# Convolution and expert layer on one core: a reordered fill, one fp16 comparison for each one-hot matrix, front work moved between half rounds, and picks spread over the last round

## The chip, the cores and the metric

One core of one Trainium2 chip. The metric is the device time of one execution in microseconds (us), shorter is better. The profile is one execution, and its span is about 1.7 us shorter than the time of that same execution.

## The reference, cut to what matters

A causal depthwise convolution of width 7 with softmaxed weights per head, then a mixture of 8 experts with top-1 routing. 28,672 tokens (8 batches of 3584) of width 192; hidden width 1024.

```python
x_pad = concat([zeros((B, 6, D)), x], axis=1)
out = einsum('hk,bskhg->bshg', softmax(weight), windows(x_pad))   # 8 heads of 24
x = out.reshape(N, D)
logits = x @ w_gate
e_idx = argmax(logits, axis=1)
gate_w = softmax(logits)[arange(N), e_idx]
eom = sigmoid(x @ w_output_gate)
for e in range(8):
    mask = e_idx == e
    h = maximum(x[mask] @ w1[e], 0.0)
    out[mask] = gate_w[mask, None] * eom[mask, e, None] * (h @ w2[e])
```

## The kernel before

The tokens are worked through in 16 units of 1792. For each unit the *front* does, on TensorE, the convolution (8 head matmuls with a band matrix), transposes and gate logits; then the routing, which counts tokens by expert and finds each token's place in its expert's stream. A unit's rows are reordered by matmuls with one-hot matrices, 8 groups of two blocks, and scattered by GpSimd (POOL in the profile) into sorted rows in device memory. The *slots* then load 512 sorted rows of one expert, transposed by the DMA, and run the two expert matmuls; results go to the output by a scatter on GpSimd. One round of the main loop is four slots of unit u interleaved with the front of later units. Units 0 to 2 go through the front before the first slot: the fill. Front convolutions and groups share two PSUM buffers (`pf`).

The front's one-hot matrices, two comparisons each with a per-row scalar:

```python
        pos = pr.tile([128, NB], FP32, tag="pos", name="pos")
        nc.vector.tensor_reduce(out=pos[P], in_=dm[P], axis=AX.X, op=ALU.add)
        # ... five small operations for dd, R, dst, du; then
        def prep(i):
            # ... (for even i: the scaled rows xr of two groups)
            pms[i] = pp16.tile([128, 2, 256], FP16, tag="pm", name="pm")
            for l in range(2):
                nc.vector.tensor_scalar(out=pms[i][P, l, :], in0=pos16[P],
                                        scalar1=pos[P, l * NG + i:l * NG + i + 1],
                                        scalar2=None, op0=ALU.is_equal)
        prep(0)
        prep(1)
```

The scatter of a group, ordered behind everything but other scatters and loads, so also behind the *guard*, eight zero writes, each over the 512 rows at the head of one expert's stream:

```python
    def scatter(u, du, xs, i):
        i = nc.gpsimd.indirect_dma_start(out=xcg2, out_offset=...(ap=du[:, i:i + 1], axis=0),
                                         in_=xs..., ...)
        nodep(i, f"sc{u}", [f"sc{v}" for v in range(NU)] + ["load"])
```

The fill and the main loop:

```python
    for u in range(U0 + 1):                       # U0 = 2
        fa, fb = front_a(u + 1, u < U0), front_b(u)
        drain(fa, 1)
        while drain(fb, 1):
            drain(fa, 2 if u < U0 else 1)
            emit_in(len(pend))                    # issue the ready row scatters
        if u == 0:
            # ... rest of fa, weights of two experts, then the guard's zero writes
    # ...
    for u in range(U0, NU):
        # ... fs: groups of unit u+1; fa, fbn: front and routing of unit u+2
        for k, (w, inv, xabi) in enumerate(todo):
            # ... weights of a later expert; s: the slot
            for q in range(4):
                pos = 4 * k + q
                if q % 2 == 0:
                    s.first(q // 2)               # half a hidden layer
                drain(fa, 1)
                if prev is not None:
                    prev.second(q)                # an output quarter of the previous slot
                    emit_out()                    # its output scatters
                if pos < 8:
                    drain(fs, 1)
                elif pos < 12:
                    drain(fa, 1)
                else:
                    drain(fbn, 1)
                emit_in(len(pend))
                # ... at pos 7 the loads of the next round
```

Within `first` the last relu of a slot's hidden layer goes to VectorE (DVE), the other three to ScalarE (ACT):

```python
                if q == 3:
                    nc.vector.tensor_relu(out=ht, in_=pps[r])
                else:
                    nc.scalar.activation(out=ht, in_=pps[r], func=AF.Relu)
```

In the last round three extra slots are *picked* on the chip (15 small VectorE operations each), all three before the round begins.

## Time and profile before

| | before |
|---|---|
| median of 4 runs, us | 647.11 (646.61 to 647.94) |
| profiled span, us | 645.5 |
| mean granted TensorE clock | 0.981 |
| VectorE, ScalarE, GpSimd busy, us | 406.3, 355.4, 401.5 |

The prediction below shows the page's first part, the stretches and the waits. Where it speaks of half clock, the granted clock of this trace is 0.50, from 65 to 68 and from 90 to 94. For the comparison afterwards four instants matter, because they cut the execution at the same points of the work in every kernel: three of TensorE and the end. This is TensorE's timeline of the kernel before (start, duration, operation; in brackets the idle time before it and what ended it): the first slot's second load being used, and the gate logits of the first and of the last of the 12 units whose logits come in a round.

```profile
90.51 0.59 PE L613 MATMUL pp<-xb,wres 128*128 128x512 f16 x1 [0.74 <-DMA xb<-xcg_sorted]
...
119.38 1.73 PE L313 MATMUL pf<-tt,wg 128*32 128x448 f32 x16
...
535.38 1.71 PE L313 MATMUL pf<-tt,wg 128*32 128x448 f32 x16 [0.42 <-DVE tt L280]
```

So the fill ends at 90.51, the first logits follow 28.87 later, the 11 rounds take 416.00 (37.82 each), and the end 645.5 - 535.38 = 110.1. These four stages are the bookkeeping of this study.

### The profile page before, as it was taken

Reading aid. Unit: us, or ns where it says so; the run is one execution under the profiler, and the core shown is the slowest. Engines: PE = TensorE matmul, PEld = TensorE weight load, DVE = VectorE, ACT = ScalarE, POOL = GpSimd, SP = SyncE. Lnnn points to the kernel's source line nnn. Section 1 sums busy time; section 2 is a strip of 40 time slices with the busy share of each in tenths; the row PEclk is TensorE's granted clock in tenths of the full one; section 3 lists DMA queues with packets and bytes.
Section 4 is the critical chain, followed back from the end, with each engine's and each line's share of the span. In section 5 each row is a group of like instructions: output and inputs, shape, how many; then the busy total and the mean of one; then the engine's idle time right before and its main releaser. Section 6 shows DMA issues by size and latency. Waiting matters only on the chain.

```text
span 645.5 us, 13578 instructions
## 1 busy us (share of the span) xinstructions
PE 586.5 (91%) x4544; PEld 360.3 (56%) x4544; DVE 406.3 (63%) x1362; ACT 355.4 (55%) x586; POOL 401.5 (62%) x419
## 2 busy tenths in 40 slices
PE   3998739999999999999999999999999999979993
PEld 1554415656665566656566566655566565546662
DVE  7567536584957658494775849577594956943332
ACT  1676525554665555556555555555555565656661
POOL 1362726876775756667476655756566674777773
PEclk9999859999999999999999999999999999999997
DMA  6979439994654647264553637355372525246631
GB/s 160 191 186 258 132 76 201 143 211 137 138 169 117 176 106 171 85 153 131 117 155 101 185 87 165 105 114 165 92 188 88 107 82 113 73 108 136 188 115 37
DMA packets 162569, 88.14 MB, mean 137 GB/s; under 512 B 116765, under 2 KB 153792, under 8 KB 162496
## 3 DMA queue, kind: packets, MB, share of 16 engines
q1 hardware_dynamic: 131872, 43.92, 30.3%
q0 software_dynamic: 29728, 43.30, 25.8%
q8 instruction: 36, 0.59, 0.4%
q14 instruction: 37, 0.30, 0.2%
q10 hardware_dynamic: 896, 0.03, 0.1%
HBM read 35.92 MB, written 43.06 MB: 122 GB/s over the span
## 4 chain that ended last, share of the span: by engine, by line
PE 66%; DVE 19%; ACT 6%; DMA 4%; issue 3%; SPq 0%; POOL 0%; DVEq 0%; ACTq 0%; POOLq 0%
PE pyt L655 18%; PE pp L613 13%; PE pf L290 11%; PE pp L620 8%; PE pf L444 5%; DVE ht L631 5%; PE pf L313 5%; PE pf L304 5%; ACT ht L633 4%; DVE xrow L423 2%; DVE pm L428 2%; DVE cv L280 2%; PE pf L322 2%; DMA out_dram<-y,oi 1%; DMA xt<-in_x_dram 1%
## 5 line engine op out<-in xcount | busy, mean ns | idle before, releaser
L482 POOL DMA_INDIRECT out_dram<-y,oi x246 | 245.6, 998 | 127.6 <-ACT y L661 63.4
L633 ACT ACTIVATE ht<-pp 128x1024 f16<-128x1024 f32 (+1 forms) x189 | 183.1, 1001 | 69.8 <-PE pp L620 67.0
L655 PEld LDWEIGHTS <-ht 128*128 128x128 f16 x1968 | 166.6, 98 | 58.2 <-issue 29.5
L655 PE MATMUL pyt<-wres,ht 128*128 128x192 f16 x1920 | 192.7, 246 | 1.5 <-DVE ht L631 1.5
L462 POOL DMA_INDIRECT xcg_sorted<-xs,du x128 | 131.5, 1027 | 92.2 <-DVE tk L502 22.1
L290 PE MATMUL pf<-xt,band 118*112 118x384 f32 x256 | 109.4, 523 | 19.1 <-DMA xt<-in_x_dram 10.8
L631 DVE TENSOR_SCALAR ht<-pp 128x1024 f16<-128x1024 f32 (+1 forms) x63 | 74.7, 1185 | 71.8 <-PE pp L613 71.8
L661 ACT COPY y<-pyt 128x384 f32<-128x384 f32 x123 | 59.0, 479 | 85.6 <-PE pyt L655 84.1
L613 PE MATMUL pp<-xa,wres 128*128 128x512 f16 x240 | 92.9, 387 | 9.1 <-DMA xa<-xcg_sorted 9.1
L613 PE MATMUL pp<-xb,wres 128*128 128x512 f16 x240 | 91.3, 380 | 1.2 <-DMA xb<-xcg_sorted 1.2
L620 PE MATMUL pp<-xb,wres 64*128 64x512 f16 x240 | 73.0, 383 | 1.6 <-ACT ht L633 1.2
L620 PE MATMUL pp<-xa,wres 64*128 64x512 f16 x240 | 73.0, 383 | 0.0
L444 PE MATMUL pf<-xrow,pm 112*128 112x194 f16 x512 | 65.1, 249 | 5.8 <-DVE pm L428 4.1
L613 PEld LDWEIGHTS <-wres 128*128 128x128 f16 x480 | 34.8, 97 | 60.7 <-issue 59.7
L290 PEld LDWEIGHTS pf<-xt,band 118*112 118x112 f32 x256 | 42.5, 185 | 41.6 <-DVE cv L280 11.5
L278 ACT COPY cv<-pf 112x384 f32<-112x384 f32 x80 | 38.1, 478 | 46.5 <-PE pf L290 38.6
L428 DVE TENSOR_SCALAR pm<-pos,pos 112x256 f16<-112x256 f16 x256 | 62.1, 307 | 0.0
L423 DVE TENSOR_TENSOR xrow<-cv,gs 112x384 f16<-112x384 f32 x121 | 61.9, 551 | 0.0
L444 PEld LDWEIGHTS <-pm 112*128 112x128 f16 x512 | 44.7, 98 | 15.3 <-DVE pm L428 7.7
L304 PE MATMUL pf<-identf,cv 112*128 112x112 f32 x384 | 50.7, 260 | 2.3 <-ACT tt L278 2.1
L278 ACT CAST xs<-pf 128x388 f16<-128x388 f32 x76 | 37.1, 492 | 27.5 <-PE pf L444 27.5
L304 PEld LDWEIGHTS pf<-identf,cv 112*128 112x128 f32 x384 | 40.9, 141 | 10.0 <-ACT tt L278 3.4
(139 smaller groups left out, 447.2 us busy)
## 6 DMA issues: line engine op xcount, KB each, us to landing
xt<-in_x_dram SPq DMA_DIRECT2D x8, 1344.0 KB
xt<-in_x_dram SPq DMA_DIRECT2D x8, 1260.0 KB
out_dram<-y,oi POOLq DMA_INDIRECT x246
wres<-in_moe_w_dram POOLq DMA_DIRECT2D x8, 384.0 KB
wd<-wres SPq DMA_DIRECT2D x3, 768.0 KB
wres<-in_moe_w_dram POOLq DMA_DIRECT2D x8, 256.0 KB
xcg_sorted<-xs,du POOLq DMA_INDIRECT x128
xcg_sorted<-zrow SPq DMA_DIRECT2D x8, 256.0 KB
```

What stands on the lines that cost most here:

```text
L278: nc.scalar.copy(out=o, in_=i)
L290: nc.tensor.matmul(pc[0:BT, 0:NB * GH], band[0:KI, h, :], xt[0:KI, :, h * GH:(h + 1) * GH], start=True, stop=True)
L304: nc.tensor.matmul(pt[:, j * BT:(j + 1) * BT], cvf[0:BT, m * 2 * D + i * 128:m * 2 * D + (i + 1) * 128], identf[0:BT, 0:BT], is_transpose= ...
L428: nc.vector.tensor_scalar(out=pms[i][P, l, :], in0=pos16[P], scalar1=pos[P, l * NG + i:l * NG + i + 1], scalar2=None, op0=ALU.is_equal)
L444: nc.tensor.matmul(ps[:, r * XW:(r + 1) * XW], pm[P, l, r * 128:(r + 1) * 128], xr[P, l * NG + i, :], start=(r == 0 and l == 0), stop=(r = ...
L462: i = nc.gpsimd.indirect_dma_start(out=xcg2, out_offset=bass.IndirectOffsetOnAxis(ap=du[:, i:i + 1], axis=0), in_=xs.rearrange("p r w -> p ...
L482: i = nc.gpsimd.indirect_dma_start(out=out, out_offset=bass.IndirectOffsetOnAxis(ap=oi[:, j:j + 1], axis=0), in_=y[:, j, :], in_offset=Non ...
L613: nc.tensor.matmul(pps[r][:, l, :], w[:, o2:o2 + 128], x, start=(r == 0), stop=(r == 1))
L620: nc.tensor.matmul(pps[r][:, l, :], w[p0:p0 + 64, c:c + 128], x[p0:p0 + 64], start=(r == 1), stop=(r == 0))
L631: nc.vector.tensor_relu(out=ht, in_=pps[r])
L633: nc.scalar.activation(out=ht, in_=pps[r], func=AF.Relu)
L655: nc.tensor.matmul(self.pp[:, o:o + D], self.ht[fc // 2][:, fc % 2, q * 128:(q + 1) * 128], self.w[:, w:w + D], start=(fc == 0 and q % 2 = ...
```

## The change

Its intent: (1) let the row scatters of unit 1 go out while the guard is still being written, and give the fill an order in which the routing of a unit starts earlier; (2) build each one-hot matrix with one instruction in place of two; (3) lay the front's pieces out over the half rounds so that logits and their transposes are separated by matmul work, and choose the copying engine by place; (4) issue weights in single pieces; (5) make one pick per slot of the last round. The core of the diff (cuts marked with ...):

```diff
-        pos = pr.tile([128, NB], FP32, tag="pos", name="pos")
-        nc.vector.tensor_reduce(out=pos[P], in_=dm[P], axis=AX.X, op=ALU.add)
+        pos = pr.tile([128, NB], FP16, tag="pos", name="pos")
+        nc.vector.tensor_reduce(out=pos[P], in_=dm[P], axis=AX.X, op=ALU.max)
 ...
-            for l in range(2):
-                nc.vector.tensor_scalar(out=pms[i][P, l, :], in0=pos16[P],
-                                        scalar1=pos[P, l * NG + i:l * NG + i + 1],
-                                        scalar2=None, op0=ALU.is_equal)
+            nc.vector.tensor_tensor(
+                out=pms[i][P], in0=bass.AP(tensor=pos16.tensor, offset=pos16.offset,
+                                           ap=[[pos16.ap[0][0], BT], [0, 2], [1, 256]]),
+                in1=pos.rearrange("p (l i) -> p i l", l=2)[P, i, :].unsqueeze(2)
+                .to_broadcast([BT, 2, 256]), op=ALU.is_equal)
 ...   (prep(0) now stands ahead of the dd, R, dst, du operations, prep(1) behind them)
-        nodep(i, f"sc{u}", [f"sc{v}" for v in range(NU)] + ["load"])
+        nodep(i, f"sc{u}", [f"sc{v}" for v in range(NU)] + ["load", "guard"])
 ...   (fill)
         while drain(fb, 1):
-            drain(fa, 2 if u < U0 else 1)
+            n += 1
+            drain(fa, 1 if u == U0 or n > 8 else 2 if n < 8 else 0)
             emit_in(len(pend))
+            if u < U0 and n > 4 and n % 2:
+                load_w(1)
 ...   (round)
-                drain(fa, 1)
+                if pos in (0, 2, 4, 6, 8, 10, 12):
+                    evac_on[0] = "act" if pos < 8 else None
+                    drain(fa, 1)
+                if pos == 14:
+                    drain(fbn, 1)
                 if prev is not None:
                     prev.second(q)
                     emit_out()
+                if pos in (1, 3, 5, 7, 8, 9, 10, 11):
+                    evac_on[0] = "dve" if pos < 8 else None
+                    drain(fa, 2 if pos == 9 else 1)
                 if pos < 8:
+                    evac_on[0] = "act"
                     drain(fs, 1)
 ...
+                if u == NU - 1 and q == 3 and k < ND:
+                    todo.append(load_pick())
```

More of the change, by code (lines that the diff above doesn't have):

```diff
@@ L202, with w_pieces, load_w @@
     wres = const.tile([128, E * WE], FP16)
-    def load_w(e):
+    def w_pieces(e):
         o = e * WE
         w = moe_w1[e]
-        nc.gpsimd.dma_start(
-            wres[:, o:o + F].rearrange("p (l c) -> p l c", l=2),
-            bass.AP(tensor=w.tensor, offset=w.offset,
-                    ap=[[F, 128], [64 * F + F // 2, 2], [1, F // 2]]))
-        nc.gpsimd.dma_start(wres[0:64, o + F:o + WA], w[0:64, F // 2:F])
-        nc.gpsimd.dma_start(wres[64:128, o + F:o + WA], w[128:D, 0:F // 2])
-        nc.gpsimd.dma_start(
-            wres[:, o + WA:o + WE].rearrange("p (c d) -> p c d", d=D),
-            moe_w2[e].rearrange("(c p) d -> p c d", p=128))
+        return [
+            (wres[:, o:o + F].rearrange("p (l c) -> p l c", l=2),
+             bass.AP(tensor=w.tensor, offset=w.offset,
+                     ap=[[F, 128], [64 * F + F // 2, 2], [1, F // 2]])),
+            (wres[0:64, o + F:o + WA], w[0:64, F // 2:F]),
+            (wres[64:128, o + F:o + WA], w[128:D, 0:F // 2]),
+            (wres[:, o + WA:o + WE].rearrange("p (c d) -> p c d", d=D),
+             moe_w2[e].rearrange("(c p) d -> p c d", p=128))]
+    wq = deque(p for e in range(E) for p in w_pieces(e))
+    def load_w(n):
+        while n and wq:
+            nc.gpsimd.dma_start(*wq.popleft())
+            n -= 1
     GE = NG * E
@@ L273, in pft @@
         return pool.tile([128, 512], FP32, tag=tag, name="pf")
+    evac_on = [None]
     def evac(o, i):
         sync_flip[0] ^= 1
-        if sync_flip[0] or fill[0] is not None:
+        if evac_on[0] is not None:
+            act = evac_on[0] == "act"
+        else:
+            act = sync_flip[0] or fill[0] is not None
+        if act:
             nc.scalar.copy(out=o, in_=i)
@@ L391, in front_b @@
                                 in1=msk[P], op=ALU.mult)
-        pos = pr.tile([128, NB], FP32, tag="pos", name="pos")
-        nc.vector.tensor_reduce(out=pos[P], in_=dm[P], axis=AX.X, op=ALU.add)
-        dd = pr.tile([128, NG, E + 1], FP32, tag="dd", name="dd")
-        nc.vector.tensor_tensor(
-            out=dd, in0=pk[:, c0 + NSEG:c0 + 2 * NSEG].rearrange("p (i e) -> p i e", e=E + 1),
-            in1=bass.AP(tensor=R9.tensor, offset=R9.offset,
-                        ap=[list(R9.ap[0]), [0, NG], [1, E + 1]]), op=ALU.add)
-        nc.vector.tensor_tensor(out=R, in0=R, in1=pk[:, c0 + 2 * NSEG:NK], op=ALU.add)
-        nc.vector.scalar_tensor_tensor(
-            out=dd, in0=pk[:, c0:c0 + NSEG].rearrange("p (i e) -> p i e", e=E + 1),
-            scalar=rowf[:, 0:1], in1=dd, op0=ALU.is_le, op1=ALU.mult)
-        dst = pr.tile([128, NG], FP32, tag="dst", name="dst")
-        nc.vector.tensor_reduce(out=dst, in_=dd, axis=AX.X, op=ALU.max)
-        du = pr.tile([128, NG], U32, tag="du", name="du")
-        nc.vector.tensor_scalar(out=du, in0=dst, scalar1=rowf[:, 0:1], scalar2=None, op0=ALU.add)
+        pos = pr.tile([128, NB], FP16, tag="pos", name="pos")
+        nc.vector.tensor_reduce(out=pos[P], in_=dm[P], axis=AX.X, op=ALU.max)
         xr = xrows[u % 2]
@@ L426, in prep @@
             pms[i] = pp16.tile([128, 2, 256], FP16, tag="pm", name="pm")
-            for l in range(2):
-                nc.vector.tensor_scalar(out=pms[i][P, l, :], in0=pos16[P],
-                                        scalar1=pos[P, l * NG + i:l * NG + i + 1],
-                                        scalar2=None, op0=ALU.is_equal)
-        prep(0)
+            nc.vector.tensor_tensor(
[3 more added lines that the diff above has]
+                .to_broadcast([BT, 2, 256]), op=ALU.is_equal)
+        prep(0)
+        dd = pr.tile([128, NG, E + 1], FP32, tag="dd", name="dd")
+        nc.vector.tensor_tensor(
+            out=dd, in0=pk[:, c0 + NSEG:c0 + 2 * NSEG].rearrange("p (i e) -> p i e", e=E + 1),
+            in1=bass.AP(tensor=R9.tensor, offset=R9.offset,
+                        ap=[list(R9.ap[0]), [0, NG], [1, E + 1]]), op=ALU.add)
+        nc.vector.tensor_tensor(out=R, in0=R, in1=pk[:, c0 + 2 * NSEG:NK], op=ALU.add)
+        nc.vector.scalar_tensor_tensor(
+            out=dd, in0=pk[:, c0:c0 + NSEG].rearrange("p (i e) -> p i e", e=E + 1),
+            scalar=rowf[:, 0:1], in1=dd, op0=ALU.is_le, op1=ALU.mult)
+        dst = pr.tile([128, NG], FP32, tag="dst", name="dst")
+        nc.vector.tensor_reduce(out=dst, in_=dd, axis=AX.X, op=ALU.max)
+        du = pr.tile([128, NG], U32, tag="du", name="du")
+        nc.vector.tensor_scalar(out=du, in0=dst, scalar1=rowf[:, 0:1], scalar2=None, op0=ALU.add)
         prep(1)
@@ L682, in chain @@
             yield from g
-    load_w(0)
-    load_w(1)
+    load_w(8)
     drain(front_a(0))
@@ L690 @@
         drain(fa, 1)
+        n = 0
         while drain(fb, 1):
-            drain(fa, 2 if u < U0 else 1)
+            n += 1
+            drain(fa, 1 if u == U0 or n > 8 else 2 if n < 8 else 0)
             emit_in(len(pend))
+            if u < U0 and n > 4 and n % 2:
+                load_w(1)
+        if u < U0:
+            drain(fa)
         if u == 0:
-            drain(fa)
-            load_w(2)
-            load_w(3)
             for e in range(E):
                 i = nc.sync.dma_start(
-                    out=xcg[e * CAP:e * CAP + TT, :].rearrange("(p g) w -> p (g w)", g=GR), in_=zrow)
+                    out=xcg[e * CAP:e * CAP + TT, :].rearrange("(p g) w -> p (g w)", g=GR),
+                    in_=zrow)
                 nodep(i, "guard", ())
-        elif u < U0:
-            drain(fa)
     def loads(u):
@@ L709, in loads, with load_pick @@
             todo.append((wres[:, e * WE:(e + 1) * WE], inv, slot_load(base, u)))
-        if u == NU - 1:
-            for sel, bap, inv in [pick(TP // 2) for _ in range(ND)]:
-                base = reg(bap[0:1, 0:1], [ET.SP], E * CAP - TT)
-                todo.append((w_dyn(sel), inv, slot_load(base, u, TT // 2)))
-        return todo
+        return todo
+    def load_pick():
+        sel, bap, inv = pick(TP // 2)
+        base = reg(bap[0:1, 0:1], [ET.SP], E * CAP - TT)
+        return w_dyn(sel), inv, slot_load(base, NU - 1, TT // 2)
     todo = loads(U0)
@@ L729 @@
             fa, fbn = front_a(u + 2), front_b(u + 2)
-        nxt = None
-        for k, (w, inv, xabi) in enumerate(todo):
-            if 0 < 4 * (u - U0) + k <= EH:
-                load_w(EH - 1 + 4 * (u - U0) + k)
+        k = 0
+        while k < len(todo):
+            w, inv, xabi = todo[k]
             s = Slot(xabi, w, inv)
@@ L736 @@
                 pos = 4 * k + q
+                if 0 <= 16 * (u - U0) + pos - 4 < 16:
+                    load_w(1)
                 if q % 2 == 0:
                     s.first(q // 2)
-                drain(fa, 1)
+                if pos in (0, 2, 4, 6, 8, 10, 12):
[3 more added lines that the diff above has]
+                    drain(fbn, 1)
                 if prev is not None:
@@ L742 @@
                     emit_out()
+                if pos in (1, 3, 5, 7, 8, 9, 10, 11):
+                    evac_on[0] = "dve" if pos < 8 else None
+                    drain(fa, 2 if pos == 9 else 1)
                 if pos < 8:
+                    evac_on[0] = "act"
                     drain(fs, 1)
-                elif pos < 12:
-                    drain(fa, 1)
-                else:
+                    evac_on[0] = None
+                    emit_in(len(pend))
+                if pos == 12:
                     drain(fbn, 1)
-                emit_in(len(pend))
+                if pos == 15:
+                    drain(fbn, 2)
                 if pos == 7 and u + 1 < NU:
                     nxt = loads(u + 1)
+                if u == NU - 1 and q == 3 and k < ND:
+                    todo.append(load_pick())
             prev = s
+            k += 1
         todo = nxt
```

## The prediction

> **What bounds the kernel now.** I read the page's first two parts, then the busy time by stretch, then the waits of the fill, then one steady round instruction by instruction.
>
> ```profile
> PE 586.5 (91%) x4544; PEld 360.3 (56%) x4544; DVE 406.3 (63%) x1362; ACT 355.4 (55%) x586; POOL 401.5 (62%) x419
> ```
>
> TensorE (PE) is busy for 91% of 645.5 us, so 59 us at most are idle. By stretch (columns: stretch, length, then busy us of PE, weight loads, DVE, ACT, POOL, then granted clock, DMA share, GB/s):
>
> ```profile
> 64.00:80.00 16.00, 12.88 (x86) 7.87 (x86) 8.67 (x38) 8.74 (x21) 12.34 (x13) 0.89 0.44 137
> 80.00:90.00 10.00, 0.88 (x3) 0.24 (x4) 5.38 (x23) 1.02 (x3) 3.90 (x4) 0.58 0.28 85
> 90.00:100.00 10.00, 8.69 (x34) 3.65 (x34) 3.88 (x14) 4.51 (x6) 1.96 (x2) 0.73 0.46 91
> ...
> 420.00:460.00 40.00, 38.34 (x311) 24.22 (x313) 27.13 (x83) 22.38 (x36) 25.85 (x27) 1.00 0.48 129
> ...
> 540.00:580.00 40.00, 35.08 (x301) 21.82 (x298) 30.09 (x128) 23.72 (x34) 28.00 (x29) 1.00 0.41 98
> ```
>
> Three places lose time: a hole of 9 us at 80 to 90, a steady state that is 96% busy, and 4.9 us lost at 540 to 580. The waits of the fill (SPq is the queue of SyncE) and the timelines of POOL and SP say where the hole comes from:
>
> ```profile
> PE pp L613 <- DMA xa<-xcg_sorted: 8.6, 1, 8.6
> ```
> ```profile
> SPq L573 <- DMA xcg_sorted<-xs,du: 19.1, 1, 19.1
> ```
> ```profile
> 49.74 0.98 POOL L213 DMA_DIRECT2D wres<-in_moe_w_dram  x1
> 63.26 1.05 POOL L462 DMA_INDIRECT xcg_sorted<-xs,du  x1 [12.54 <-DVE du L407]
> ...
> 83.83 0.98 POOL L462 DMA_INDIRECT xcg_sorted<-xs,du  x1 [0.31 <-issue]
> ```
> ```profile
> 46.78 7.06 SPq L699 DMA_DIRECT2D xcg_sorted<-zrow  x8
> ...
> 86.60 1.23 SPq L573 DMA_TRANSPOSE xa<-xcg_sorted  x1
> ```
>
> The first expert slot waits for its transposed load; that waits for the last scatter of unit 2, started at 83.83. POOL needs 1.29 us per scatter (0.98 plus 0.30) and has 16 to do from 63.26 on, back to back. Unit 1's first rows were copied out of PSUM at 49.7, so POOL stood 12.5 us. The line names the tile du, but unit 1's du was ready at 47.5; in that time eight zero writes (the guard, 2 MB, issued 46.8 to 53.8) were moving, and the old scatter is ordered behind them. I choose to read the wait as the guard's.
>
> In the steady state one round is one unit of front work and four slots. The large L313 blocks at 119.45 and 535.38 are 11 rounds apart: 37.8 us each. From stretches without a wait I get the pure TensorE stream: 8 half hidden layers at 1.51, 16 output quarters at 0.66, 8 convolutions at 0.65, 6 transpose groups at 0.39, 1.66 for the gate logits, 0.48 for their transposes, 0.56 for the counting matmuls, 8 groups at 0.335: 12.1 + 10.6 + 5.2 + 2.3 + 1.7 + 0.5 + 0.6 + 2.7 = 35.6. So a round loses 2.2 us, and 12 rounds 26 us: the ceiling there. What loses it is the DVE:
>
> ```profile
> 438.00 0.47 DVE L428 TENSOR_SCALAR pm<-pos,pos 112x256 f16<-112x256 f16 x2
> 438.39 1.22 DVE L631 TENSOR_SCALAR ht<-pp 128x1024 f16<-128x1024 f32 x1
> 439.52 0.55 DVE L280 COPY cv<-pf 112x384 f32<-112x384 f32 x1
> ```
> ```profile
> 440.13 0.90 PE L290 MATMUL pf<-xt,band 118*112 118x384 f32 x2 [0.74 <-DVE cv L280]
> ```
>
> A convolution needs one of two PSUM buffers; its copy-out stands in DVE's queue behind one-hot matrices and a 1.2 us relu. DVE runs without a pause from 427.5 to 442.3 in this round.
>
> [...] The new comparison broadcasts pos[...]. No trace of the kernel before shows this case; the nearest, the product of 112x384 with a broadcast gs (fp32 inputs), takes 0.47 us from start to start[...]. [...]
>
> **Part by part.**
>
> *Guard.* Unit 1's scatters no longer wait for it and go out from about 50, mixed with four weight pieces (0.6 to 0.98 us each), done near 61. Unit 2's rows are copied out from 65.4 to 73.8. With 1.29 per scatter the last starts at about 65.5 + 7 x 1.29 = 74.5, not 83.8. The load chain from there to the first whole hidden matmul took 90.5 - 83.8 = 6.7 us, so data are there at 81.2. TensorE's other work ended at 80.6. Gain: 90.5 - 81.2 = 9.3 us.
>
> *Fill order.* The last gate step gets one group between it and the logits; the first one-hot no longer waits behind five small DVE operations on dd and du (1.1 us). TensorE waits of 1.0 (57.2) and 1.8 us (64.1) for pm should shrink, and with them a stretch of half clock at 65 to 68; I count 1.7 us. Sum of the fill: 11 us.
>
> *The one comparison.* Removed: two comparisons per group, 0.39 us together (438.00 to 438.39). Added: one of 512 results [...] 0.60 us (a record near 0.67). That is 0.21 us more for each of 128 groups, 27 us more DVE work in all, 1.7 us a round. So fewer instructions but more time, in the very stretch where DVE is the bound.
>
> *Who copies out.* Convolutions alternate ACT and DVE by place, group rows go to ACT. Before, a round put 8 copies of either kind on DVE (8 x 0.48 = 3.8 us net); now 4 (1.9 us). So DVE gains 1.9 and pays 1.7: its total per round stays. ACT gets about 1.9 us more at 22.4 of 40 busy: hidden.
>
> *Half round.* Logits and their transposes are now separated by a half hidden layer, which removes the waits for tt, lt (0.6 and 0.2 us at 459.7 and 462.2). But the routing of the next unit starts later: the gb copy moves behind a hidden half, the counting step moves from the 14th to the 15th of 16 places and stands behind a relu. Laying both queues out by hand from the durations above, with 0 where the 13th place starts: pos is ready at 8.4 (6.6 before), the first one-hot at 10.05, the counting tile's PSUM is free at 10.75, against TensorE's arrival at 9.9. I find waits of 0.4 (count), 0.9 (first group), 0.4 (fifth convolution): 1.7 us a round in place of 2.2. Gain 0.5 x 12 = 6 us. With the old comparisons the same layout would wait about 0.6.
>
> *Spread picks.* Three picks of 15 DVE operations ran as one block from 561.4 to 569.6; TensorE idled 1.18 and 1.52 us:
>
> ```profile
> 561.00:572.00 11.00, 8.30 (x70) 4.95 (x69) 9.51 (x53) 6.00 (x8) 8.28 (x9) 1.00 0.21 73
> ```
>
> One per slot of the last round, 2.75 us beside 5.7 us of TensorE work where DVE has 1.7 to do: hidden. Gain 2.7 us, all of that window's idle time.
>
> *Weight pieces.* One at a time instead of four. POOL is not on the steady path: 0.
>
> Sum: 11 + 6 + 2.7 = about 20; 647.3 - 20 = 627; I say 628.
>
> **Rivals.**
> 1. *The slower comparison eats the steady gain or more.* For: DVE is continuous over half a round and the layout has three waits on it. Each 0.1 us of error per group is 0.8 us a round, 10 us in all. Then steady is 5 us worse than before and the time is about 638.
> 2. [...] 0.34 us, less than the old pair: waits of 0.6 a round, gain 19 us there, time about 614. [...]
> 3. *The guard hole is filled by another wait.* TensorE's own chain ends at 80.6, so if the scatters of unit 2, weights and zero writes share the DMA engines (share above 1.15 from 50 to 65) and land late, half of the 9 us goes. Time about 632. Against it: the share falls to 0.2 to 0.3 after 70.
> 4. *Half clock.* With only 0.9 us of matmul between 77.3 and 80.6 the first slot may still start at half clock; I have counted no gain from the clock there[...].
>
> **Range and chances.** The fill and the picks (about 14 us) are well supported; the steady part may be -8 to +16. That makes 618 to 638. 2% is 634.4, i.e. a gain of 13: the fill and the picks alone just reach it. Faster 0.77, same 0.22, slower 0.01.
>
> **What would show it.** Right: POOL's first scatter of unit 1 near 50; first hidden matmul near 81; the comparison near 0.67 us, 128 times; DVE busy near 405 to 410; a period of 37.0 to 37.5 us; no PE idle from picks. Wrong: comparisons near 0.4; a period above 37.8 with waits for pm; a hole still wider than 4 us before the first slot.

## The result, and the profile after

| | before | after |
|---|---|---|
| median of 4 runs, us | 647.11 | 629.1 (627.09 to 631.29) |
| profiled span, us | 645.5 | 625.4 |
| granted clock | 0.981 | 0.982 |

The ratio is 0.9721 (95%: 0.9687 to 0.9755), all runs in the fast state: 2.8% faster. A ratio here is the mean time of one kernel's fast runs over that of the other's of the same rounds, so not quite the ratio of the medians. The profiled execution of after was the fastest of its four (627.09), so the spans differ by 20.1 where the medians differ by 18.0.

The page of the kernel after, first part:

```profile
PE 575.0 (92%) x4544; PEld 359.1 (57%) x4544; DVE 404.1 (65%) x1182; ACT 382.5 (61%) x638; POOL 416.6 (67%) x419
```

VectorE has 180 instructions fewer and is busy nearly as long. ScalarE has 27 us more, as more copies go to it, and GpSimd 15 us more, which the prediction had not foreseen: GpSimd issues the same transfers. TensorE's timeline of the kernel after, at the same instants:

```profile
82.75 0.58 PE L627 MATMUL pp<-xa,wres 128*128 128x512 f16 x1 [5.29 <-DMA xa<-xcg_sorted]
83.83 0.59 PE L627 MATMUL pp<-xb,wres 128*128 128x512 f16 x1 [0.49 <-DMA xb<-xcg_sorted]
...
110.92 1.71 PE L326 MATMUL pf<-tt,wg 128*32 128x448 f32 x16
147.54 1.71 PE L326 MATMUL pf<-tt,wg 128*32 128x448 f32 x16
...
514.80 1.71 PE L326 MATMUL pf<-tt,wg 128*32 128x448 f32 x16
```

Differences of these instants give the account:

| stage | before, us | after, us | change |
|---|---|---|---|
| start to first slot's second load in use | 90.51 | 83.83 | -6.7 |
| from there to the first logits in a round | 28.87 | 27.09 | -1.8 |
| 11 rounds between logits | 416.00 | 403.88 | -12.1 |
| last logits to the end | 110.1 | 110.6 | +0.5 |
| sum | 645.5 | 625.4 | -20.1 |

The total stands where the prediction put it, but not its parts: the fill gave less, the rounds twice as much, the end nothing. The stretches of the kernel after (columns as in the prediction) show the first two:

```profile
80.00:90.00 10.00, 6.56 (x24) 2.44 (x26) 3.94 (x14) 3.40 (x5) 0.98 (x1) 0.62 0.37 71
...
420.00:460.00 40.00, 39.29 (x318) 25.26 (x317) 28.47 (x82) 25.47 (x41) 27.77 (x27) 1.00 0.51 133
```

The hole is there still, 5.3 us wide ahead of the load of the first slot and at a low clock (0.62), and the steady rounds are now 98% busy where they were 96%. The stretch of 540 to 580 is no longer the same work and is not compared.

The costliest one-hot groups by form, before and then after (busy us and mean ns of one, then the idle time before them):

```profile
L428 DVE TENSOR_SCALAR pm<-pos,pos 112x256 f16<-112x256 f16 x256 | 62.1, 307 | 0.0
```
```profile
L426 DVE TENSOR_TENSOR pm<-pos,pos 112x512 f16<-112x512 f16 x128 | 86.7, 682 | 0.0
```

The one comparison takes 682 ns where two took 614 (their records overlap; busy time is 62.1 and 86.7), for 128 groups 25 us more. That is close to the prediction, 27 us more and a record near 0.67 us.

What is left in a steady round are two waits. These are TensorE's waits in the round from 441.45, then what VectorE and ScalarE did there:

```profile
450.02 0.23 PE L398 MATMUL pf<-lsum,np 64*128 64x128 f16 x1 [0.32 <-DVE og L384]
453.63 0.49 PE L458 MATMUL pf<-xrow,pm 112*128 112x194 f16 x4 [0.40 <-DVE dd L435]
```
```profile
448.07 1.23 DVE L645 TENSOR_SCALAR ht<-pp 128x1024 f16<-128x1024 f32 x1 [0.44 <-PE pp L627]
449.21 0.14 DVE L377 TENSOR_SCALAR nu<-pf 64x1 uint32<-64x1 f32 x1
449.39 0.14 DVE L379 TENSOR_SCALAR nu<-nu 64x1 uint32<-64x1 uint32 x1
449.57 0.39 DVE L382 CAST np<-nu 64x128 f16<-64x128 uint32 x1
...
452.46 0.68 DVE L426 TENSOR_TENSOR pm<-pos,pos 112x512 f16<-112x512 f16 x1
```
```profile
451.27 1.94 ACT L647 ACTIVATE ht<-pp 128x1024 f16<-128x1024 f32 x2 [0.35 <-PE pp L634]
453.10 0.48 ACT L291 COPY cv<-pf 112x384 f32<-112x384 f32 x1
```

The first wait is for the counts (np), whose three small operations stand behind a 1.23 us relu. The second is put down to a dd operation, but the first one-hot was ready at 453.14 and the matmul began at 453.63, just after ScalarE ended the copy of the first convolution (453.10 + 0.48): TensorE waited for that copy to free a PSUM buffer. The profile itself says so elsewhere: in the eight rounds from 221.5 on it lays this wait seven times to ScalarE's copy (`PE pf L458 <- ACT cv L291: 2.8, 7, 0.4`) and once to dd. The copy had to wait for two relus. So neither wait is for the comparison.

### The profile page after: what moved, and what is told of

Its sections match the earlier page's. It is cut to its first block, busy times and chain, and to the rows that moved or that the text cites. A ratio compares the mean times of both kernels' runs of the same rounds, so it can differ in the third digit from the quotient of the medians.

```text
span 625.4 us, 13450 instructions
## 1 busy us (share of the span) xinstructions
PE 575.0 (92%) x4544; PEld 359.1 (57%) x4544; DVE 404.1 (65%) x1182; ACT 382.5 (61%) x638; POOL 416.6 (67%) x419
## 4 chain that ended last, share of the span: by engine, by line
PE 80%; DVE 8%; ACT 5%; DMA 4%; issue 2%; POOL 0%; SPq 0%; ACTq 0%; POOLq 0%; DVEq 0%
PE pyt L669 22%; PE pp L627 18%; PE pf L303 12%; PE pp L634 10%; PE pf L458 6%; PE pf L317 6%; PE pf L326 5%; ACT ht L647 3%; DVE ht L645 2%; DMA xb<-xcg_sorted 1%; DVE pm L426 1%; PE pf L335 1%; ACT cv L291 1%; DMA out_dram<-y,oi 1%; DVE band L142 1%
## 5 line engine op out<-in xcount | busy, mean ns | idle before, releaser
L496 POOL DMA_INDIRECT out_dram<-y,oi x246 | 253.1, 1029 | 116.4 <-issue 56.4
L476 POOL DMA_INDIRECT xcg_sorted<-xs,du x128 | 138.4, 1081 | 69.1 <-ACT xs L291 31.7
L303 PE MATMUL pf<-xt,band 118*112 118x384 f32 x256 | 105.4, 507 | 11.0 <-DVE band L142 10.6
L291 ACT CAST xs<-pf 128x388 f16<-128x388 f32 x128 | 61.7, 486 | 52.1 <-PE pf L458 50.0
L426 DVE TENSOR_TENSOR pm<-pos,pos 112x512 f16<-112x512 f16 x128 | 86.7, 682 | 0.0
L458 PE MATMUL pf<-xrow,pm 112*128 112x194 f16 x512 | 63.3, 247 | 11.2 <-DVE pm L426 5.7
L458 PEld LDWEIGHTS <-pm 112*128 112x128 f16 x512 | 44.6, 97 | 37.6 <-issue 15.3
L291 ACT COPY cv<-pf 112x384 f32<-112x384 f32 x80 | 38.1, 479 | 22.1 <-PE pf L303 21.9
L317 PE MATMUL pf<-identf,cv 112*128 112x112 f32 x384 | 49.3, 259 | 0.7 <-ACT cv L291 0.7
L293 DVE COPY cv<-pf 112x384 f32<-112x384 f32 x48 | 26.6, 553 | 29.1 <-PE pf L303 28.2
```

Source lines behind the costliest of these rows:

```text
L291: nc.scalar.copy(out=o, in_=i)
L303: nc.tensor.matmul(pc[0:BT, 0:NB * GH], band[0:KI, h, :], xt[0:KI, :, h * GH:(h + 1) * GH], start=True, stop=True)
L317: nc.tensor.matmul(pt[:, j * BT:(j + 1) * BT], cvf[0:BT, m * 2 * D + i * 128:m * 2 * D + (i + 1) * 128], identf[0:BT, 0:BT], is_transpose= ...
L426: nc.vector.tensor_tensor(out=pms[i][P], in0=bass.AP(tensor=pos16.tensor, offset=pos16.offset, ap=[[pos16.ap[0][0], BT], [0, 2], [1, 256]] ...
L458: nc.tensor.matmul(ps[:, r * XW:(r + 1) * XW], pm[P, l, r * 128:(r + 1) * 128], xr[P, l * NG + i, :], start=(r == 0 and l == 0), stop=(r = ...
L476: i = nc.gpsimd.indirect_dma_start(out=xcg2, out_offset=bass.IndirectOffsetOnAxis(ap=du[:, i:i + 1], axis=0), in_=xs.rearrange("p r w -> p ...
```

## The experiments

Theory A, at the outset: the guard's wait, the order in the rounds and the comparison each act as the prediction has them, the comparison costing VectorE time in the rounds. Rival B: the comparison's cost and the picks' gain lie beside other work; what sets the fill and the end is GpSimd's queue. All twelve kernels gave correct results. Times are medians of four runs; the kernel before took 646.88 on the chip of e1, e2, e4 and e5, and 647.98 on that of e3b, e9b, e8 and e10.

### e1: the kernel after with two comparisons

```diff
-        pos = pr.tile([128, NB], FP16, ...)
+        pos = pr.tile([128, NB], FP32, ...)
-            nc.vector.tensor_tensor(out=pms[i][P], in0=<pos16 twice>, in1=<pos broadcast>, op=ALU.is_equal)
+            for l in range(2):
+                nc.vector.tensor_scalar(out=pms[i][P, l, :], in0=pos16[P],
+                                        scalar1=pos[P, l * NG + i:l * NG + i + 1],
+                                        scalar2=None, op0=ALU.is_equal)
```

> The changed kernel with the two comparisons per group of before (fp32 position as a pointer scalar); all else as changed. Both theories: DVE busy falls by about 25 us, from 404 to 379, since the one comparison is busy 86.7 us and the two were 62.1. Theory A (of the prediction: the slower comparison stands on the path of a round): the period from one gate-logits block to the next falls from 36.7 to 35.9 to 36.3 us, and the time from 629 to 619 to 625. Rival B (the DVE wave of the new round order has slack): the period stays at 36.5 to 36.7 and the time at 626 to 630.

624.84 us (624.14 to 625.72), ratio 0.9651 (0.9616 to 0.9686): the single comparison makes the kernel some 3 to 4 us slower (4.3 against the kernel after, on another chip; 2.8 on the same chip against e5, the kernel after with the old picks). VectorE's busy time falls to 380.6, as both theories had it. The time lies in theory A's range, but the period in rival B's: the last eight rounds take 36.67 us each in both kernels. The first difference is at the first slot, whose second load is in use at 80.58 here and at 83.83 in the kernel after. GpSimd's timeline of the kernel after, around unit 1's first scatter and unit 2's last:

```profile
48.25 5.66 POOL L476 DMA_INDIRECT xcg_sorted<-xs,du  x1 [1.32 <-ACT xs L291]
...
76.99 1.19 POOL L476 DMA_INDIRECT xcg_sorted<-xs,du  x1 [0.30 <-issue]
```

The same first scatter in e1:

```profile
48.95 1.08 POOL L475 DMA_INDIRECT xcg_sorted<-xs,du  x1 [1.17 <-ACT xs L291]
50.01 1.15 POOL L221 DMA_DIRECT2D wres<-in_moe_w_dram  x1
```

One scatter took 5.66 us in place of 1.08. VectorE ran this, from the kernel after and then from e1:

```profile
48.56 1.27 DVE L426 TENSOR_TENSOR pm<-pos,pos 112x512 f16<-112x512 f16 x2
49.76 0.54 DVE L422 TENSOR_TENSOR xrow<-cv,gs 112x384 f16<-112x384 f32 x1
50.23 1.28 DVE L426 TENSOR_TENSOR pm<-pos,pos 112x512 f16<-112x512 f16 x2
51.44 1.01 DVE L422 TENSOR_TENSOR xrow<-cv,gs 112x384 f16<-112x384 f32 x2
52.38 0.67 DVE L426 TENSOR_TENSOR pm<-pos,pos 112x512 f16<-112x512 f16 x1
```
```profile
49.02 0.86 DVE L427 TENSOR_SCALAR pm<-pos,pos 112x256 f16<-112x256 f16 x4
49.80 0.54 DVE L422 TENSOR_TENSOR xrow<-cv,gs 112x384 f16<-112x384 f32 x1
```

In the kernel after VectorE reads two operands from on-chip memory in every instruction from before the scatter's start until 53.05, and the scatter ends at 53.9, soon after the first pause. In e1 the comparisons have one such operand and the scatter takes 1.08 us. The pattern repeats: the same scatter takes 5.66 to 5.67 us in e5, e6 and e7, which have the one comparison and the freed guard too, and 1.16 and 1.19 in e8 and e10, which have two. The next scatter is the longer one with two comparisons: 1.90 us in e1 and 2.90 in e8 and e10, against 1.04 in the kernel after. A run of two-operand instructions alone does not make a scatter long: in the kernel after itself unit 0's first three, at 32.99, 35.21 and 36.73, took 1.17 to 1.22 us, beside operations with two such operands that follow each other from 32.21 to 37.64. So it is shown that this scatter is long with the one comparison and short with two; what makes one scatter long and another not stays open.

A part of e1's gain is given back: its third round waits for a load, and the two rounds from 144.60 to 222.14 take 77.54, 4.2 us more than two steady ones (73.86 in the kernel after, 0.5 more). From the last logits to the end it is 108.5 us, 2.1 shorter than after; here the comparison does stand on the path, as TensorE waits 2.6 us for one-hot matrices in the kernel after and 1.4 in e1. These parts (-3.3, +3.7, -2.1, and 0.3 left before the first logits) sum to the spans' difference of -1.4, while the medians differ by 4.3; the profiled run of after was the fastest of its kernel and that of e1 the slowest. The size of 3 to 4 us is the timed rounds' and is not divided up in full.

### e2: the kernel before with the one comparison

The same edit in reverse, with the `max` reduction, and nothing else.

> The kernel before with only the one comparison put in. Theory A: in the old round order DVE is the bound for half a round, 8 x 0.2 us more of it lengthens the period of 37.8 by 0.6 to 1.4 us and the time by 8 to 17, to 655 to 664. Rival B: there is slack, the time stays within 3 us of 647.

656.16 us (655.46 to 656.94), ratio 1.0138 (1.0101 to 1.0175). Eleven rounds take 422.4 us here (120.94 to 543.36), 38.40 each, against 37.82 in the kernel before. So in the old order VectorE's longer work does lie on the path: 0.6 us a round, some 7 us of the 9 in 12 rounds (1.7 more lie ahead of the first slot, 1.1 at the end). Theory A holds for the old order, B for the new: the same instruction costs nothing in the steady rounds of the kernel after, where the waits that remain are on other things.

### e3b and e3: the kernel before with only the guard freed

```diff
-        nodep(i, f"sc{u}", [f"sc{v}" for v in range(NU)] + ["load"])
+        nodep(i, f"sc{u}", [f"sc{v}" for v in range(NU)] + ["load", "guard"])
```

> The kernel before with one edit: the scatters no longer wait for the zero writes. Theory A (that wait alone is the fill's gain): the first slot starts 6 to 9 us earlier than 90.5, the time is 638 to 641. Rival B (without the spread weight pieces the 8 pieces and the zero writes keep the DMA engines full and the scatters land late): less than 4 us, 643 to 647.

e3 ran on a chip on which every kernel was slow; the kernel before too took 768.95 us (750.93 to 776.55), at a granted clock of 0.92 to 0.93. e3 took 755.94, three of its four runs in the slow state: no verdict. It was run again as e3b:

> Repeat of e3, whose chip ran every kernel 15 to 19% slow. The kernel before with one edit: the scatters no longer wait for the zero writes. Theory A (that wait alone is the fill's gain): first slot 6 to 9 us earlier than 90.5, time 638 to 641. Rival B (eight weight pieces and the zero writes keep the DMA engines full and the scatters land late): under 4 us, 643 to 647.

641.29 us (640.31 to 643.17), ratio 0.9906 (0.9874 to 0.9939): 6.7 us. The first slot's second load is in use at 83.69, against 90.51; the last scatter starts at 77.02, against 83.83. Its rounds are the old ones (two of them from 453.21 to 528.83, 37.8 each). The guard alone thus gives as much as the fill gave in the kernel after; that the two agree is chance, as e9b shows below.

### e4: the kernel after with the guard's wait put back

The reverse of the same line.

> The changed kernel with the scatters ordered behind the zero writes again; all else as changed. Theory A (the wait for the zero writes made the hole): unit 1's first scatter goes from 48 back to 60 or later, the first slot starts 5 to 8 us later than 83.8, the time is 634 to 638. Rival B (POOL's 16 scatters, four weight pieces and DMA traffic set the hole anyway): the first slot moves by less than 2 us, the time is 628 to 631.

635.85 us (635.12 to 637.58), ratio 0.9833 (0.9794 to 0.9871): 6.8 us longer than the kernel after by the medians of two chips, 8.2 longer than e5 on the same chip. GpSimd's timeline of e4 shows the wait, at 58.99 where 60 or later was expected. By the edit it is the guard's, though the line names another tile, as it did before:

```profile
58.99 0.98 POOL L476 DMA_INDIRECT xcg_sorted<-xs,du  x1 [12.46 <-DVE dm L402]
```

The last scatter starts at 82.71 and the first slot's loads are in use at 88.35 and 89.69. The reading of the prediction, guard and not du, is confirmed from both sides.

### e5: the kernel after with the three picks in one block

The picks are made in `loads` for the last round, as in the kernel before; the pick per slot is taken out.

> The changed kernel with the three picks in one block at the load of the last round, as before. Theory A (of the prediction): TensorE loses 2.7 us to the block, the time is 631 to 633. Rival B (what TensorE loses there it has to wait anyway for the last scatters, which stand in POOL's queue behind output scatters): the block shifts no end, the last round's first hidden matmul comes at the same time within 0.5 us, the time is 628 to 630.

627.68 us (626.48 to 630.35), ratio 0.9704 (0.966 to 0.9748), so no slower than the kernel after. Spreading the picks was worth nothing. Yet the block does stop TensorE in e5, for as long as the prediction had it, when a relu stands behind the picks in VectorE's queue:

```profile
552.20 0.37 PE L634 MATMUL pp<-xb,wres 64*128 64x512 f16 x1 [2.64 <-DVE ht L645]
```

This pause puts off TensorE's own work, so that the load of the last round, issued at 552.77, is there when TensorE comes to it: no wait for it shows. In the kernel after it is the other way round. First GpSimd and SyncE in the kernel after, then TensorE:

```profile
548.20 0.98 POOL L476 DMA_INDIRECT xcg_sorted<-xs,du  x1 [0.30 <-issue]
```
```profile
550.69 1.14 SPq L587 DMA_TRANSPOSE xa<-xcg_sorted  x1
```
```profile
553.96 0.39 PE L627 MATMUL pp<-xa,wres 128*128 128x512 f16 x1 [1.57 <-DMA xa<-xcg_sorted]
555.00 0.41 PE L627 MATMUL pp<-xb,wres 128*128 128x512 f16 x1 [0.65 <-DMA xb<-xcg_sorted]
```

The last unit's rows are scattered between output scatters, 1.29 us each; the load of the last round is ordered behind the last of them, and TensorE waits for the load. In the kernel before the same chain ran from 569.45 over 572.27 to the matmul at 576.57, and the picks' block lay in the time in which that chain was under way. So the block's wait (2.64 us) and the chain's (1.57 + 0.65 us) cover one another, and taking one away uncovers the other. In the kernel after the clock falls there as well, to a mean of 0.67 from 556 to 560 (0.50 from 556 to 558); in e1, with waits of 2.31 and 0.46 us at the same place, it stays at 1.00. TensorE ran 26 matmuls in these 4 us against 36 in e1: by that count, an estimate, about 1.1 of e1's 2.1 us at the end.

### e6, e7 and e9: three further edits, on the slow chip

e6 holds the output scatters back in the first half of the last round but one (`if u != NU - 2 or pos >= 8: emit_out()`). e7 issues four of the fill's weight pieces after unit 2's scatters instead of between those of unit 1 and 2. e9 is the kernel after with the whole old fill: old order, weights at the old places, the guard's wait.

> The changed kernel, in the last round but one the output scatters of the first two slots are held back until the unit's row scatters are out. Theory B of the picks (POOL's queue sets the start of the last round): the last row scatter starts at about 541 instead of 548, TensorE's wait of 3.2 us at 552 and the half clock after it go, the time falls by 3 to 5 us to 624 to 626. Rival: y buffers now fill up and TensorE or ACT waits for them, no gain or a loss, 628 to 632.

> The changed kernel with the four weight pieces of expert 3 issued after unit 2's row scatters instead of between unit 1's. If POOL's queue sets the hole of 5.8 us before the first slot (four pieces are 3.0 us of issue): the last row scatter starts at 73 to 75 instead of 77, the first slot 2 to 4 us earlier, the time 625 to 627. If the scatter that took 5.7 us at 48 waits for DMA traffic of zero writes and inputs that stays: under 1.5 us, 628 to 630.

> The changed kernel with the old fill: old order of steps, weights of experts 2 and 3 in one block after unit 0, scatters behind the zero writes. Rounds, comparison and picks as changed. If fill and rounds add up: the first slot starts at about 90, 6 to 7 us later than 83.8, the period is 36.7 as in the changed kernel, the time 635 to 637. If the new fill also shortened the rounds: over 640.

They shared the slow chip with e3: 725.92, 728.65 and 727.3 us, ratios 0.9642, 0.9641 and 0.9656, each with an interval 2.6 to 2.8% wide, which covers all that was to be told apart. Nothing follows about their sizes. e9 was repeated, e6 and e7 went into e8.

### e9b: the kernel after with the old fill, on a fast chip

> Repeat of e9, whose chip was slow. The changed kernel with the whole old fill (order, weights in a block, scatters behind the zero writes). If fill and rounds add up: first slot near 90 with a period of 36.7, time 634 to 637, as with the wait alone put back (635.9); then order and spread pieces are worth under 2 us. If they are worth more, 638 or above.

636.6 us (636.41 to 636.79), ratio 0.9825 (0.9797 to 0.9853). First slot at 91.57, no better than before; rounds of 36.67. So the rounds without the fill are worth 1.75%, the guard without the rounds (e3b) 0.94%, and 0.9825 x 0.9906 = 0.9733, close to the 0.9721 of the whole change: the two parts add up. Against e4 (635.85, new order with the wait) the fill's new order and the single weight pieces are worth 0.8 us by medians of two chips, 1.9 us by the instant of the first slot (91.57 against 89.69). With the guard freed they are worth more. The kernels to compare are e3b and e1, both with two comparisons: 83.69 with the old order, 80.58 with the new, 3.1 us. These are the two lines:

```profile
83.69 0.59 PE L613 MATMUL pp<-xb,wres 128*128 128x512 f16 x1 [0.51 <-DMA xb<-xcg_sorted]
```
```profile
80.58 0.58 PE L626 MATMUL pp<-xb,wres 128*128 128x512 f16 x1 [0.73 <-DMA xb<-xcg_sorted]
```

In the kernel after the long scatter takes 3.25 us back (83.83), which is why its fill looks like that of the freed guard alone.

### e8: two comparisons, held output scatters and late weight pieces together

The edits of e1, e6 and e7.

> The changed kernel with the two comparisons (as e1), the four weight pieces of expert 3 after unit 2's scatters, and the row scatters of the last unit ahead of the output scatters. If POOL's queue sets both the fill's hole and the start of the last round: the last scatter of unit 2 starts at 70 to 72 (73.9 in e1), the first slot at 78 to 79.5 (80.6), the last unit's scatters end 6 to 8 us earlier against the last gate block and TensorE no longer waits for the last round's load, time 618 to 621. If not: 623 to 626. The period stays 36.67 in either case.

624.74 us (624.04 to 625.96), ratio 0.9646 (0.9616 to 0.9677): no better than e1 alone (624.84), so the expectation was missed. The trace shows why the sum did not come. The last scatter of the fill starts earlier (71.35, against 73.89 in e1), and the load is issued earlier (73.90, against 76.66), but its data are in use only at 80.60 and 82.43, against 79.27 and 80.58: 6.70 us from issue to first use, against 2.61. In between GpSimd issued the four weight pieces at 72.3 to 75.1. That these pieces are what makes the load late is argued from that timing and was not shown; a version with early scatters and the weights left in place was not run. At the end the wait for the last round's load is gone (the last row scatter starts at 540.03), but the end is not shorter: 109.0 us from the last logits, 108.5 in e1. TensorE does finish earlier (94.8 us after these logits, 97.8 in e1), but GpSimd, which from 560 on issues scatter after scatter with some 0.3 us between them, starts the last output scatter 6.4 us after TensorE's end, against 2.9 in e1. The output scatters that were held back came due in that queue; this is read from its timeline, and no run tests it.

### e10: e8 with one relu on ScalarE and the hold in two early rounds too

```diff
-                if q == 3:
+                if q == 3 and not act:
                     nc.vector.tensor_relu(out=ht, in_=pps[r])
 ...
-                    s.first(q // 2)
+                    s.first(q // 2, pos == 14)
 ...
-                    if u != NU - 2 or pos >= 8:
+                    if u not in (U0, U0 + 1, NU - 2) or pos >= 8:
                         emit_out()
```

The relu is the one ahead of the counts in VectorE's queue.

> As e8, and two edits more: the DVE's relu in the last slot of each round goes to ACT, so that the count of the next unit doesn't stand behind it; and the output scatters of the second round's first two slots are held back too. Theory (the 1.1 us that a round still loses are the count waiting behind that relu and the first group waiting for a copy-out behind two relus on ACT): the wait for the count, 0.3 us, goes, the period falls from 36.67 to 35.9 to 36.3, the extra 1 to 4 us of the third round go, time 610 to 616. Rival (ACT becomes late instead and the wait for the first group grows): period 36.6 or more, 618 to 622.

612.21 us (611.01 to 613.62), ratio 0.9442 (0.9413 to 0.9471): 12.5 us better than e8 and the best version found. TensorE's timeline of e10: the two logits that frame the steady rounds, and, in a steady round, the two instructions that waited in the kernel after.

```profile
146.62 1.71 PE L326 MATMUL pf<-tt,wg 128*32 128x448 f32 x16
...
503.92 1.71 PE L326 MATMUL pf<-tt,wg 128*32 128x448 f32 x16
```
```profile
440.64 0.23 PE L398 MATMUL pf<-lsum,np 64*128 64x128 f16 x1
...
443.69 0.50 PE L457 MATMUL pf<-xrow,pm 112*128 112x194 f16 x4
```

Ten rounds take 357.30 us, 35.73 each, against the 35.6 that the prediction had added up as the pure TensorE stream; neither instruction waits. A round is 0.94 us shorter than in e8 (36.67); the two waits were 0.72 of it (0.32 + 0.40, in the round of the kernel after), and the rest is not laid to anything. Whether the first group's wait went with the relu or with something else in e10 is not separated. The bump of the early rounds is gone as well: the row scatters of that round end behind the one that starts at 139.53 (149.67 in e1), because output scatters no longer stand between them, and the rounds from 110.89 to 182.35 take 35.73 each too. But in e8, without that early hold, the bump was only 0.2 us (36.84 from 146.63 to 183.47), and the eleven rounds together take 393.0 us against 403.4: 10.4 of the 10.6 us by which the spans differ. They come in every round, and so hardly from the hold in the early ones.

## Why the prediction was right

The time was 629.1 against 628 predicted, inside the range. By its own steps:

- **Guard, -9.3 us, and fill order, -1.7: too large, measured -6.7 together up to the first slot.** The mechanism is right (e3b: 6.7 us for that one line). What the sum left out is what the new comparison does to GpSimd: the last scatter, "65.5 + 7 x 1.29 = 74.5", started at 76.99, and unit 1's were done at 66.9, not "near 61". In e1, with two comparisons, the last starts at 73.89 and the first slot's second load is in use at 80.58: the two steps give 9.9 us there, against 11. Of these the guard is 6.8 (e3b) and the order, with the single pieces, 3.1 (e1 against e3b), so the first was put too large and the second too small. The half clock at 65 to 68 (0.50) is gone as predicted: 1.00 from 55 to 70 in the kernel after.
- **One comparison, 0.60 us apart and a record near 0.67: right**, 0.60 from start to start (two begin at 48.56, and what follows them at 49.76) and 0.68. VectorE's busy time, predicted at 405 to 410, is 404.1, just below. The 0.60 was the author's estimate; by proportion to the 0.47 us for 384 results that the trace of the kernel before shows, an estimate too, 512 would have been 0.63. Rival 2 (0.34 us, the author's estimate as well) is out.
- **The comparison's effect in the rounds, 1.7 us of VectorE work a round and waits of 1.7 us where two comparisons would leave 0.6: wrong.** In the new order it costs nothing there (36.67 with either form), while in the old it costs 0.6 a round (e2). The moved copies and the separated logits are what is left to explain the gain; they were not tested apart.
- **Rounds, 0.5 us each, 6 us: too small, 1.10 each by the mean of 11 (37.82 to 36.72), 12 us in all, and 1.8 up to the first.** The mis-sized term is the sum of three waits laid out by hand, 1.7 us. Measured: 0.32 for the counts (0.4 predicted), 0.40 for the first group (0.9), none for the fifth convolution (0.4). The second was laid to VectorE; it is ScalarE's copy behind two relus, in the queue that the prediction called hidden. The 35.6 us of pure stream held: e10 reaches 35.73.
- **Picks, -2.7 us: failed, measured +0.5 for the whole end, and e5, with the block put back, is no slower.** The block's own cost was right (2.64 us in e5). The step took "all of that window's idle time" for the block's. Behind the block stood the chain of the last row scatter, the load and the first matmul, which had been hidden.
- **Rival 3** (another wait fills the guard's hole) came in part: 5.3 us of hole remained, over the 4 that the prediction named as a sign against itself. The wait was in GpSimd's queue; that the load's landing was not late is seen from its own time, 2.8 us from issue (79.96) to use (82.75). Rival 4's half clock is there: 0.50 from 82 to 86 in the kernel after, 0.62 over 80 to 90.

So the total was right because a fill and an end that gave less (8.5 us with the leg to the first logits, minus 0.5, against 13.7) met rounds that gave 12 against 6. That the two errors cancel is luck. The range has a slip too: with 13.7 us and a steady part of -8 to +16 it would reach to 642, not 638.

## What to carry to other kernels

Read each stage's gain from its own instants, before and after: here a right total hid wrong terms of opposite sign. An instruction's price depends on the wait that ends last where it stands: the same longer comparison cost 0.6 us a round in one order, nothing in another, and 3 us in the fill, where one scatter of another engine ran long beside it (5.66 us against 1.08). Compare kernels that differ in one thing: the new fill order looked worthless (83.69 against 83.83) until the comparison was held fixed (83.69 against 80.58). A queue that carries two kinds of transfers is a schedule of its own: in e8, where output scatters were held back, the wait at the start of the last round (2.31 and 0.46 us in e1) is gone, and the last output scatter starts 6.4 us after TensorE's end, against 2.9. Moving one relu from in front of a short chain, with output scatters held back in two early rounds, gave more (12.5 us) than the spread picks and the new fill order together.
